# A three-part layer on one core: chunk loads over all partitions, values in one layout, and other tile shapes in the chunk products

## The chip, the cores and the metric

The kernel runs on one core of a Trainium2 chip. The time is device microseconds of that core, the median of three runs; lower is better.

## The reference

Three parts run one after the other on B, S = 4 sequences of 768 tokens, model width 384. First a gated recurrence with 8 heads of width 48, then causal attention in which 4 experts share one input and each token keeps 2 of them, then an MLP with a normalisation. All of it is fp32.

```
state = alpha[:, :, t, :, None] * state + einsum('bhd,bhde->...', k_t, v_t)   # outer product k v
y[:, :, t] = einsum('bhd,bhde->bhe', q_t, state)
...
q, k, v = x @ wq[e], x @ wk[e], x @ wv[e];  a = softmax(causal(q k^T / 8))
out += (e in top 2) * w * ((a @ v) @ wo[e])
...
xn = (x - mu) / sqrt(var + 1e-6) * g_ln;  out = x + relu(xn @ w_ch1) @ w_ch2
```

The change touches the first part alone.

## The kernel before

**The recurrence in chunks.** Each sequence is cut into 6 chunks of 128 tokens, 24 chunks in all, numbered c, with s = c % 6. The 8 heads are 4 pairs: j counts the pairs and h the two heads of a pair. A chunk's alpha, q and k lie in one tile `ld` (four buffers, 128 partitions x 1540 words): head h has partitions 64h to 64h + 47, and the 16 partitions behind them hold ones. The steps of a chunk are:

- `load_sc` (L107) brings alpha, q and k in two transfers of 48 partitions. The ones come once, at the start, in eight transfers of 16 partitions that ACT issues (L132). `load_vn` and `load_vb` bring the same values v twice: `vn` in full and `vb` with one head of the pair in each half of the key rows and zeros elsewhere.
- `gla_a` (L203): DVE scans alpha into the running product `gt` (L215), ACT forms 1/gt by Ln and Exp (L217, L218), DVE and POOL scale k and q by it (L219 to L222).
- `gla_b` (L230): PE forms the scores inside the chunk (L240), DVE masks them into `smk` (L241), PE transposes k (L246) and ACT copies it to `kt` (L248). For scores of head h, the 128 keys are split into two halves of 64, since the second half of the keys meets only the last 64 queries.
- `gla_c` (L252): PE multiplies `kt` by v into the new state (L264), DVE and POOL add it to the old one and scale it (L271 to L274), PE forms the outputs Y from `smk` and v and from q and the old state `st` (L291), ACT and DVE split Y into `xh` and `xl` (L301, L302).

For each two chunks `qkv` projects `xh` and `xl` to the attention's q, k and v (L318, L333). `split_w` (L186) splits the projection weights into WH on ACT and WL on DVE; it runs once, near the start.

**The rest.** Attention goes by units of one 128-query block and one pair of experts: `scores` (L451 on PE, L459 and L463 behind it), `transp` (L485), `av` (L509), `wout` (L522). While the units of the first three sequences run, `conv` splits the MLP's weights, from loads `raw` on SP (L544). The MLP runs last, in `mlp_1` (L642) and `mlp_2` (L659).

**What sets the order.** `front` is a generator that yields an estimated PE time after each step; attention pulls from it so that the chunks are spread between the units. In iteration c of `front` come gla_a(c + 2), gla_b(c + 1), gla_c(c), then the loads for later chunks, then steps of `qkv`. A scheduler then orders each engine's instructions from its own estimate of times; each engine runs its own in that order. All loads but the ones, w1hl and the stores stand in one queue on SP, and an entry there that waits holds up those behind it. PSUM tiles come from one pool of 8 banks (`psf`).

On PE a matmul of fp32 operands is two instructions, and one of fp32r operands is one.

Of the kernel before, what the change touches and what calls it, by code (L numbers as in the profile page):

```python
# [10 lines left out]
F32 = mybir.dt.float32  # L11
# [20 lines left out]
SB = 0  # L32
# [39 lines left out]
def kernel(ctx: ExitStack, tc: tile.TileContext, akq, vt, vd, wqkv, wo, g_ln, w1, w2, ones, out):  # L72
# [30 lines left out]
    vn = [gl.tile([128, 4, 3, 2, 16], F32, name=f"vn{i}") for i in range(3)]  # L103
    vb = [gl.tile([128, 2, 4, 3, 2, 16], F32, name=f"vb{i}") for i in range(2)]
    st = [gl.tile([128, 4, 3, 2, 16], F32, name=f"st{i}") for i in range(2)]

    def load_sc(c):  # L107
        b, s = divmod(c, NSC)
        t = ld[c % 4]
        for h in range(2):  # L110
            sp.dma_start(t[64 * h:64 * h + 48, :], akq[b, s, h])

    def load_vn(c):
        b, s = divmod(c, NSC)
        sp.dma_start(vn[c % 3].rearrange("p j u h e -> p (j u h e)"), vt[b, s])

    def load_vb(c):
        b, s = divmod(c, NSC)
        sp.dma_start(vb[c % 2].rearrange("p x j u h e -> p (x j u h e)"), vd[b, s])
# [26 lines left out]
    load_vn(2)  # L146
# [15 lines left out]
    gmask = gl.tile([128, 192], F32, name="gmask")  # L162
    pool.memset(gmask, -1.0)
    for h in range(2):
        for c0, n in ((0, 128), (128, 64)):
            m = gmask[64 * h:64 * h + 64, c0:c0 + n]
            pool.affine_select(out=m, in_=m, pattern=[[1, n]], compare_op=OP.is_ge, fill=0.0, base=0,
                               channel_multiplier=-1)
# [83 lines left out]
    def gla_c(c):  # L252
        s = c % NSC
        q, k = qk_of(c)
        if s < NSC - 1:
            P = psf()[:, :384].rearrange("p (j u h e) -> p j u h e", j=4, u=3, h=2)
            kt = G.pop((c, "kt"))
            for j in range(4):
                if SB:
                    for h in range(2):  # L260
                        r = slice(64 * h, 64 * h + 64)
                        pe.matmul(P[r, j, :, h, :], kt[:, j, r], vn[c % 3][:, j, :, h, :], start=True, stop=True)
                else:
                    pe.matmul(P[:, j].rearrange("p u h e -> p (u h e)"), kt[:, j, :],  # L264
                              vn[c % 3][:, j].rearrange("p u h e -> p (u h e)"), start=True, stop=True)
            new = st[(c + 1) % 2]
            for h in range(2):
                r = slice(64 * h, 64 * h + 48)
                gl_b = G[c][r, :, 128:129, None].to_broadcast([48, 4, 3, 16])
                if s == 0:  # L270
                    dve.tensor_tensor(new[r, :, :, h, :], P[r, :, :, h, :], gl_b, op=OP.mult)  # L271
# [557 lines left out]
```

## Time and profile before

| | us |
|---|---|
| median of 3 runs (771.96 to 774.6) | 773.7 |
| the profiled execution, its own time | 773.15 |
| span of the profiled execution, first to last instruction | 771.4 |
| PE busy | 719.9 |
| DVE busy | 450.1 |
| ACT busy | 309.9 |
| POOL busy | 186.8 |

Busy times come from the profiled execution. A busy PE counts the modelled ends of pipelined matmuls, so it is not a PE at its peak; how fast matmuls follow each other is read from their start times. What a wait costs is read from the chain of work that ended last, which the page follows back from the last instruction, and from the stage in which the wait stands.

### The profile page before, as it was taken

To read this page: it belongs to the slowest core of one execution; us is meant where nothing else is said; L and a number is where in the kernel's file an instruction comes from. 1 tells how busy PE (TensorE), PEld (TensorE's weight loads), DVE (VectorE), ACT (ScalarE), POOL (GpSimd) and SP (SyncE) were. 2 spreads that over 40 slices of the span, in tenths; PEclk is the share of its full clock that TensorE was granted. 3 is DMA by queue.
4 is the path that set the end of the run, shared out by engine and by line. 5 is a ranking of instruction groups with operands and counts; after the bars stand their busy time and mean duration, and the time that the engine had idled before them with its cause. 6 is when DMAs were issued, how large, how long until landed. Compare 5 with 4: busy or idle time off the path is not lost.

```text
span 771.4 us, 16732 instructions
## 1 busy us (share of the span) xinstructions
PE 719.9 (93%) x6600; PEld 651.6 (84%) x6600; DVE 450.1 (58%) x1349; ACT 309.9 (40%) x903; POOL 186.8 (24%) x311
## 2 busy tenths in 40 slices
PE   3788799889998999999899999999999999999998
PEld 3777588768786778788766898999999999999997
DVE  2767677776877777765579983343354335424521
ACT  2333455544554564545467662331232123222310
POOL 4444345333544424432324320000000000000000
PEclk8697899999999999999999999999999999999999
DMA  9852524345354444221553311011011101110000
GB/s 168 220 146 80 137 92 131 104 109 125 98 161 110 118 121 114 70 85 51 188 210 93 94 52 52 22 31 42 11 33 42 42 11 31 42 39 14 31 21 22
DMA packets 31711, 64.84 MB, mean 84 GB/s; under 512 B 3856, under 2 KB 20752, under 8 KB 31632
## 3 DMA queue, kind: packets, MB, share of 16 engines
q1 hardware_dynamic: 21936, 48.81, 23.6%
q10 hardware_dynamic: 8608, 10.23, 4.4%
q0 software_dynamic: 1088, 4.72, 1.7%
q8 instruction: 52, 0.85, 0.5%
q14 instruction: 27, 0.22, 0.1%
HBM read 49.59 MB, written 14.16 MB: 83 GB/s over the span
## 4 chain that ended last, share of the span: by engine, by line
PE 74%; DMA 11%; DVE 9%; issue 2%; ACT 1%; POOL 1%; SPq 1%; ACTq 0%; DVEq 0%; POOLq 0%
PE F L659 20%; PE F L642 20%; DMA ld<-in_akq_dram 8%; PE F L509 5%; PE F L318 5%; PE F L291 4%; PE F L485 4%; PE F L240 4%; PE F L451 3%; PE F L522 3%; PE F L333 2%; PE F L264 2%; DMA xt<-xs 2%; PE F L246 1%; PE F L623 1%
## 5 line engine op out<-in xcount | busy, mean ns | idle before, releaser
L646 ACT ACTIVATE hh<-F 128x256 fp32r<-128x256 f32 x144 | 54.9, 384 | 202.0 <-PE F L642 201.5
L642 PE MATMUL F<-nh,w1hl 128*128 128x256 f32 x864 | 129.1, 285 | 0.8 <-ACT at L488 0.7
L642 PEld LDWEIGHTS F<-nh,w1hl 128*128 128x128 f32 x864 | 114.7, 191 | 3.1 <-issue 1.0
L659 PE MATMUL F<-w2h,hh 128*128 128x384 f32 x288 | 98.7, 343 | 0.0
L659 PE MATMUL F<-w2l,hh 128*128 128x384 f32 x288 | 97.8, 339 | 0.0
L659 PE MATMUL F<-w2h,hl 128*128 128x384 f32 x288 | 97.7, 339 | 0.0
L647 DVE SCALAR_TENSOR_TENSOR hl<-F,hh 128x256 fp32r<-128x256 f32 x144 | 60.0, 420 | 53.8 <-ACT hh L646 53.7
L463 ACT ACTIVATE A<-F,nm 128x384 f32<-128x384 f32 (+4 forms) x128 | 68.4, 542 | 50.8 <-DVE nm L461 22.8
L663 DVE TENSOR_TENSOR xt<-F,xt 128x384 f32<-128x384 f32 x24 | 13.4, 558 | 112.6 <-PE F L659 112.6
L642 PE MATMUL F<-nl,w1hl 128*128 128x256 f32 x432 | 75.5, 283 | 0.0
L509 PE MATMUL F<-at,V 128*64 128x128 f32 x672 | 59.7, 290 | 5.6 <-DVE rb L511 3.6
L642 PEld LDWEIGHTS F<-nl,w1hl 128*128 128x128 f32 x432 | 62.2, 192 | 0.2 <-DVE cva L548 0.2
L509 PEld LDWEIGHTS F<-at,V 128*64 128x64 f32 x672 | 41.0, 140 | 19.3 <-issue 5.6
L240 PE MATMUL F<-ld 48*64 48x128 f32 (+1 forms) x768 | 44.4, 261 | 13.7 <-DVE ld L221 13.7
L485 PE MATMUL F<-ident,A 128*128 128x128 f32 x336 | 54.2, 283 | 1.9 <-DVE smk L241 1.1
L240 PEld LDWEIGHTS F<-ld 48*64 48x64 f32 x768 | 38.4, 142 | 20.4 <-issue 16.1
L659 PEld LDWEIGHTS F<-w2l,hh 128*128 128x128 f32 x288 | 54.1, 188 | 0.4 <-issue 0.4
L659 PEld LDWEIGHTS F<-w2h,hh 128*128 128x128 f32 x288 | 54.1, 188 | 0.5 <-issue 0.4
L659 PEld LDWEIGHTS F<-w2h,hl 128*128 128x128 f32 x288 | 54.0, 188 | 0.2 <-issue 0.2
L459 DVE CUSTOM_DVE_ANT_0 F<-F,cmask 128x384 f32<-128x384 f32 (+4 forms) x96 | 46.4, 518 | 4.0 <-PE F L451 3.6
L215 DVE TENSOR_TENSOR_SCAN gt<-ld,hot 128x516 f32<-128x516 f32 (+1 forms) x26 | 30.1, 1166 | 30.6 <-DMA ld<-in_akq_dram 20.3
L222 POOL TENSOR_TENSOR ld<-ld,gt 128x512 f32<-128x512 f32 (+1 forms) x26 | 29.8, 1148 | 69.2 <-DVE gt L215 45.9
(246 smaller groups left out, 1433.3 us busy)
## 6 DMA issues: line engine op xcount, KB each, us to landing
ld<-in_akq_dram SPq DMA_DIRECT2D x48, 288.8 KB, 5.8
vb<-in_vd_dram SPq DMA_DIRECT2D x24, 384.0 KB, 3.7
vn<-in_vt_dram SPq DMA_DIRECT2D x24, 192.0 KB, 2.7
raw<-in_w_dram SPq DMA_DIRECT2D x18, 256.0 KB, 2.7
wsc<-whl ACTq DMA_DIRECT2D x18, 256.0 KB, 2.6
xs<-xo ACTq DMA_DIRECT2D x24, 192.0 KB, 1.9
w1hl<-wsc POOLq DMA_DIRECT2D x4, 1152.0 KB, 12.0
raw<-in_w_dram SPq DMA_DIRECT2D x12, 384.0 KB, 3.2
```

The costliest lines, as they stand in the source:

```text
L215: dve.tensor_tensor_scan(gt[:, js].rearrange("p j t -> p (j t)"), al[:, 129 * j0:129 * j1], hot[:, js].rearrange("p j t -> p (j t)"), 0.0, ...
L240: pe.matmul(P[64 * h:64 * h + 64, a, c0:c0 + n], k[r, j, s0:s0 + 64], q[r, j, t0:t0 + n], start=True, stop=True)
L291: pe.matmul(l[x][2], l[x][0], l[x][1], start=(x == 0), stop=(x == n - 1), skip_group_check=True)
L318: pe.matmul(P, wt[:, k, cs], x[:, k], start=(n == 0), stop=(n == 8))
L459: dve.tensor_tensor_reduce(t, t, cmask[:, 512 - pw:], -1.0, 3e38, OP.add, OP.min, m)
L463: act.activation(A[h][:, pw * x:pw * x + pw], t, AF.Exp, bias=nm[:, h:h + 1], scale=1.0 if x < npc - 1 else -1.0, accum_out=dn2[:, h, x:x ...
L485: pe.transpose(P[:, 128 * n:128 * n + 128], A[h][:, 128 * x:128 * x + 128], ident)
L509: pe.matmul(O[64 * h:64 * h + 64, :], V[:, x, HD * e:HD * e + HD], at[:, c:c + 128], start=(x == 0), stop=(x == i), skip_group_check=True)
L642: pe.matmul(P, w[:, k, c], x[:, k], start=(n == 0), stop=(n == 8))
L646: act.activation(hh, P, AF.Relu)
L647: dve.scalar_tensor_tensor(hl, P, 0.0, f(hh), op0=OP.max, op1=OP.subtract)
L659: pe.matmul(P, x[:, o], w[:, ff], start=(ff == 0 and n == 0), stop=(ff == KF - 1 and n == 2))
```

## The change

Values are loaded once, 128 keys on 128 partitions: for each pair j a block x = 0 with the first 32 columns of v of both heads, and a block x = 1 with the last 16 columns of head h in place h of 32 and zeros beside them. `vn` is gone and `vb` has three buffers of 128x512 words in place of two of 128x768. The ones are part of `akq` in memory, so `ld` arrives in one transfer of 128 partitions and ACT issues no load at the start. A chunk's scores are eight matmuls with 48 rows and 128 columns of weights, two heads side by side in two PSUM banks, and the masked scores have 128x512 words per head in place of four blocks of 192 columns. The state product has 128 moving columns in place of 96, and the state is kept in blocks of 32 columns. All outputs are 32 columns of weights wide, four of them side by side. `perm` orders the rows of the projection weights to match.

```diff
     def load_sc(c):
         b, s = divmod(c, NSC)
-        t = ld[c % 4]
-        for h in range(2):
-            sp.dma_start(t[64 * h:64 * h + 48, :], akq[b, s, h])
-
-    def load_vn(c):
-        b, s = divmod(c, NSC)
-        sp.dma_start(vn[c % 3].rearrange("p j u h e -> p (j u h e)"), vt[b, s])
+        sp.dma_start(ld[c % 4], akq[b, s])
...
-    for i in range(4):
-        for cs in ((slice(0, AW), slice(AW, CW)) if i == 0 and AF0 else (slice(0, CW),)):
-            for h in range(2):
-                act.dma_start(ld[i][64 * h + 48:64 * h + 64, cs], ones[:, cs])
-                if i < 2:
-                    sp.dma_start(ld[i][64 * h:64 * h + 48, cs], akq[0, i, h][:, cs])
+    for i in range(2):
+        load_sc(i)
     for i in range(2):
         load_vb(i)
-        load_vn(i)
-        if i == 0:
-            load_sc(2)
...
-    load_vn(2)
+    load_sc(2)
+    load_vb(2)
     load_sc(3)
...
-        SM[c] = gw.tile([128, 4, 192], F32, name="smk")
-        for j0 in (0, 2):
-            P = psf()[:, :384].rearrange("p (j t) -> p j t", j=2)
-            for a in range(2):
-                j = j0 + a
-                for c0, n, s0, t0 in ((0, 128, 0, 0), (128, 64, 64, 64)):
-                    for h in range(2):
-                        r = slice(64 * h, 64 * h + 48)
-                        pe.matmul(P[64 * h:64 * h + 64, a, c0:c0 + n], k[r, j, s0:s0 + 64], q[r, j, t0:t0 + n], start=True, stop=True)
-            dve.tensor_tensor(SM[c][:, j0:j0 + 2], P, gmask[:, None, :].to_broadcast([128, 2, 192]), op=OP.mult)
-            yield 850
+        SM[c] = gw.tile([128, 2, 4, 128], F32, name="smk")
+        P = [psf().rearrange("p (j t) -> p j t", j=4) for h in range(2)]
+        for j in range(4):
+            for h in range(2):
+                r = slice(64 * h, 64 * h + 48)
+                pe.matmul(P[h][:, j], k[r, j], q[r, j], start=True, stop=True)
+            if j == 1:
+                yield 850
+        for h in range(2):
+            dve.tensor_tensor(SM[c][:, h], P[h], gmask[:, None, :].to_broadcast([128, 4, 128]), op=OP.mult)
+        yield 850
...
-                    pe.matmul(P[:, j].rearrange("p u h e -> p (u h e)"), kt[:, j, :],
-                              vn[c % 3][:, j].rearrange("p u h e -> p (u h e)"), start=True, stop=True)
+                pe.matmul(P[:, 128 * j:128 * j + 128], kt[:, j, :], v[:, j].rearrange("p x h e -> p (x h e)"), start=True, stop=True)
+            P = P.rearrange("p (j b e) -> p j b e", j=4, b=4)
...
+                bs = slice(h, 3, 2 - h)
...
-                    dve.tensor_tensor(new[r, :, :, h, :], st[c % 2][r, :, :, h, :], P[r, :, :, h, :], op=OP.add)
-                    (dve if GST else pool).tensor_tensor(new[r, :, :, h, :], new[r, :, :, h, :], gl_b, op=OP.mult)
+                    dve.tensor_tensor(new[r, :, bs], st[c % 2][r, :, bs], P[r, :, h::2], op=OP.add)
+                    (dve if GST else pool).tensor_tensor(new[r, :, bs], new[r, :, bs], gl_b, op=OP.mult)
...
-                l = [(bd[:, 0, j].rearrange("p u h e -> p (u h e)")[:, cs], SM[c][:, j, 0:128], o),
-                     (bd[:, 1, j].rearrange("p u h e -> p (u h e)")[:, cs], SM[c][:, j, 128:192], o[:, 64:128])]
-                if s:
-                    l.append((sto[:112, j, cs], q[:112, j, :], o))
...
         for T in range(2):
-            grp([(2 * T + a, slice(0, 64), Y[64 * a:64 * a + 64, T, :]) for a in range(2)])
+            jobs = []
+            for n in range(4):
+                j, h = 2 * T + n // 2, n % 2
+                l = [(v[:, j, 0, h], sm[:, h, j])]
+                if s:
+                    l.append((sto[:112, j, h], q[:112, j]))
+                jobs.append((Y[32 * n:32 * n + 32, T], l))
+            grp(jobs)
             yield 800
-        grp([(j, slice(64, 96), Y[32 * j:32 * j + 32, 2, :]) for j in range(4)])
+        jobs = []
+        for j in range(4):
+            l = [(v[:, j, 1, h], sm[:, h, j]) for h in range(2)]
+            if s:
+                l.append((sto[:112, j, 2], q[:112, j]))
+            jobs.append((Y[32 * j:32 * j + 32, 2], l))
+        grp(jobs)
...
-            if c + 2 < NCH:
-                load_vb(c + 2)
             if c + 3 < NCH:
-                load_vn(c + 3)
+                load_vb(c + 3)
```

The scheduler's order moves with it. In rows of it, a name's number tells the buffer (`ld_83` is the `ld` of chunks 0, 4, 8 and so on, `ld_85` that of 2, 6, 10), what follows it is the shape, and the last number is how many times in a row. Line numbers are those of the kernel that the row is of. SP's queue at the start of the program, before:

```order
L134 DMA ld_83<-in_akq_dram 48x1540 x2
L134 DMA ld_84<-in_akq_dram 48x1540 x2
L119 DMA vb_90<-in_vd_dram 128x768
L115 DMA vn_87<-in_vt_dram 128x384
L111 DMA ld_85<-in_akq_dram 48x1540 x2
L119 DMA vb_91<-in_vd_dram 128x768
L115 DMA vn_88<-in_vt_dram 128x384
L144 DMA A<-in_wqkv_dram 128x772 x3
L115 DMA vn_89<-in_vt_dram 128x384
L111 DMA ld_86<-in_akq_dram 48x1540 x2
```

And of the changed kernel:

```order
L108 DMA ld_83<-in_akq_dram 128x1540
L108 DMA ld_84<-in_akq_dram 128x1540
L112 DMA vb_87<-in_vd_dram 128x512
L112 DMA vb_88<-in_vd_dram 128x512
L130 DMA A<-in_wqkv_dram 128x772 x3
L108 DMA ld_85<-in_akq_dram 128x1540
L112 DMA vb_89<-in_vd_dram 128x512
L108 DMA ld_86<-in_akq_dram 128x1540
L136 DMA gsb<-in_g_ln_dram 128x3
```

The load of chunk 2 has moved behind the three weight tiles. DVE's order a little later, around the scan (L215) and last product (L221) of chunk 2, before:

```order
L215 SCALAR_TENSOR_TENSOR gt<-ld_85,hot 128x516
L221 SCALAR_TENSOR_TENSOR ld_83<-ld_83 128x256
L220 TENSOR_TENSOR ld_84<-ld_84,gi 128x256
L221 SCALAR_TENSOR_TENSOR ld_83<-ld_83 128x256
L221 SCALAR_TENSOR_TENSOR ld_84<-ld_84 128x256 x2
L241 TENSOR_TENSOR smk<-F,gmask 128x384
L220 TENSOR_TENSOR ld_85<-ld_85,gi 128x512
L189 TENSOR_TENSOR WL<-A,WH 128x772
L241 TENSOR_TENSOR smk<-F,gmask 128x384
L221 SCALAR_TENSOR_TENSOR ld_85<-ld_85 128x512
```

And of the changed kernel, where L199, L204 and L205 are the scan and the two products and L225 is the mask:

```order
L173 TENSOR_TENSOR WL<-A,WH 128x772
L225 TENSOR_TENSOR smk<-F,gmask 128x512 x2
L173 TENSOR_TENSOR WL<-A,WH 128x772
L199 SCALAR_TENSOR_TENSOR gt<-ld_85,hot 128x516
L225 TENSOR_TENSOR smk<-F,gmask 128x512 x2
L252 TENSOR_TENSOR st_91<-F,gt 48x4x2x32
L252 TENSOR_TENSOR st_91<-F,gt 48x4x64
L204 TENSOR_TENSOR ld_85<-ld_85,gi 128x512
L287 TENSOR_TENSOR xl<-F,xh 128x3x128
L199 SCALAR_TENSOR_TENSOR gt<-ld_86,hot 128x516
L205 SCALAR_TENSOR_TENSOR ld_85<-ld_85 128x512
```

The scan of chunk 2 stands behind all of the weight splits now, and its last product behind chunk 1's masks and state and chunk 3's scan. On PE, one chunk in the middle of a sequence (chunk 4), from the last of its scores to its outputs, before:

```order
L240 MATMUL F<-ld_83 64x64 x2
L246 MATMUL F<-ident,ld_83 128x128 x4
L264 MATMUL F<-vn_87,kt 128x96 x4
L291 MATMUL F<-smk,vb_91 64x128 x2
L291 MATMUL F<-smk,vb_91 64x64 x2
L291 MATMUL F<-ld_86,st_93 64x128 x2
L291 MATMUL F<-smk,vb_91 64x128 x2
L291 MATMUL F<-smk,vb_91 64x64 x2
L291 MATMUL F<-ld_86,st_93 64x128 x2
L291 MATMUL F<-smk,vb_91 32x128 x4
L291 MATMUL F<-smk,vb_91 32x64 x4
L291 MATMUL F<-ld_86,st_93 32x128 x4
```

And of the changed kernel (the shape is that of the output; L221, L230, L244 and L263 stand for L240, L246, L264 and L291):

```order
L221 MATMUL F<-ld_83 128x128 x8
L230 MATMUL F<-ident,ld_83 128x128 x4
L244 MATMUL F<-vb_87,kt 128x128 x4
L263 MATMUL F<-smk,vb_87 32x128 x4
L263 MATMUL F<-ld_86,st_91 32x128 x4
L263 MATMUL F<-smk,vb_87 32x128 x4
L263 MATMUL F<-ld_86,st_91 32x128 x4
L263 MATMUL F<-smk,vb_87 32x128 x8
L263 MATMUL F<-ld_86,st_91 32x128 x4
```

The scores come as eight matmuls where sixteen stood, and the 64-column outputs and the products with 64 moving columns are gone.

## Rows read from the trace of the kernel before

**Rows 1.** The page's chain that ended last: share of the span by engine.

```profile
PE 74%; DMA 11%; DVE 9%; issue 2%; ACT 1%; POOL 1%; SPq 1%; ACTq 0%; DVEq 0%; POOLq 0%
```

**Rows 2.** Windows: us, busy of PE, PEld, DVE, ACT, POOL, clock, DMA, GB/s.

```profile
0.00:25.00 25.00, 8.78 (x56) 8.39 (x56) 9.97 (x14) 6.82 (x13) 11.54 (x27) 0.80 0.96 214
...
50.00:92.00 42.00, 31.71 (x374) 26.84 (x373) 30.23 (x86) 15.83 (x46) 20.09 (x30) 0.85 0.52 129
92.00:372.00 280.00, 265.79 (x3030) 223.49 (x3029) 203.12 (x626) 142.16 (x422) 110.55 (x190) 0.98 0.39 105
```

**Rows 3.** Chain in order of time: start us, us, what.

```profile
2.18 10.26 DMA ld<-in_akq_dram
12.46 8.02 DMA ld<-in_akq_dram
...
39.38 4.61 PE F L318 x36
...
50.76 7.18 DMA ld<-in_akq_dram
...
75.46 6.51 DMA ld<-in_akq_dram
...
260.18 5.64 DMA ld<-in_akq_dram
```

**Rows 4.** Timeline of the start: start us, us, instruction, idle before and releaser.

```profile
0.85 11.46 ACTq L132 DMA_DIRECT2D ld<-in_ones_dram  x8
...
8.17 1.28 DVE L215 TENSOR_TENSOR_SCAN gt<-ld,hot 128x258 f32<-128x258 f32 x2 [8.17 <-DMA ld<-in_ones_dram]
...
12.36 0.73 ACT L217 ACTIVATE gi<-gt 128x258 f32<-128x258 f32 x2 [10.26 <-DMA ld<-in_ones_dram]
...
22.41 1.54 PE L240 MATMUL F<-ld 48*64 48x128 f32 x16 [12.59 <-DVE ld L221]
```

**Rows 5.** The page's DMA issues: count, KB each, us to landing.

```profile
ld<-in_akq_dram SPq DMA_DIRECT2D x48, 288.8 KB, 5.8
...
vn<-in_vt_dram SPq DMA_DIRECT2D x24, 192.0 KB, 2.7
```

**Rows 6.** Windows of two stretches at the start, columns as in rows 2.

```profile
3.00:15.00 12.00, 6.82 (x40) 6.58 (x38) 2.86 (x5) 2.20 (x7) 4.87 (x13) 1.00 1.04 186
20.50:25.00 4.50, 1.54 (x16) 1.39 (x16) 4.40 (x5) 2.74 (x4) 2.57 (x2) 0.50 1.10 400
```

**Rows 7.** Window from the first scan to chunk 3's scan.

```profile
8.10:34.70 26.60, 12.93 (x148) 11.75 (x148) 18.16 (x27) 8.31 (x16) 10.68 (x10) 0.68 0.94 215
```

**Rows 8.** Waits: who for whom, us in total, times, longest.

```profile
DVE gt L215 <- DMA ld<-in_akq_dram: 20.3, 9, 3.4
```

**Rows 9.** Timeline of PE in two stretches.

```profile
191.87 0.28 PE L451 MATMUL F<-KH,QL 64*128 64x128 f32 x2
191.98 0.28 PE L451 MATMUL F<-KL,QH 64*128 64x128 f32 x2
...
258.13 0.54 PE L291 MATMUL F<-smk,vb 128*32 128x128 f32 x16
258.48 0.41 PE L291 MATMUL F<-ld,st 112*32 112x128 f32 x8
```

**Rows 10.** Chain in order of time, 250 to 262 us.

```profile
252.78 1.49 PE F L240 x32
...
254.85 0.87 PE F L264 x8
```

**Rows 11.** Window of the PE stage, instructions of L240 alone.

```profile
92.00:372.00 280.00, 30.09 (x544) 25.61 (x544) 0.98 0.39 105
```

**Rows 12.** Chain of the PE stage, shares by line.

```profile
by line: DMA ld<-in_akq_dram 11.2%; PE F L318 9.8%; PE F L291 8.8%; PE F L509 8.4%; PE F L240 6.4%; PE F L485 6.1%; PE F L451 5.7%; PE F L333 5.1%; PE F L522 4.6%; PE F L264 3.9%; issue 3.3%; PE F L246 2.1%; DMA raw<-in_w_dram 2.0%; DVE F L
```

**Rows 13.** Groups by form, 0 to 440 us: busy us, mean ns.

```profile
L241 DVE TENSOR_TENSOR smk<-F,gmask 128x384 f32<-128x384 f32 x48 | 25.9, 548 | 1.2 <-PE F L240 0.9
...
L490 DVE COPY at<-F 128x512 f32<-128x512 f32 x17 | 11.6, 682 | 0.4 <-PE F L485 0.3
```

More of the change, by code (lines that the diff above doesn't have):

```diff
@@ L71, with kernel @@
 @with_exitstack
-def kernel(ctx: ExitStack, tc: tile.TileContext, akq, vt, vd, wqkv, wo, g_ln, w1, w2, ones, out):
+def kernel(ctx: ExitStack, tc: tile.TileContext, akq, vd, wqkv, wo, g_ln, w1, w2, out):
     nc = tc.nc
@@ L102 @@
     ld = [gl.tile([128, CW], F32, name=f"ld{i}") for i in range(4)]
-    vn = [gl.tile([128, 4, 3, 2, 16], F32, name=f"vn{i}") for i in range(3)]
-    vb = [gl.tile([128, 2, 4, 3, 2, 16], F32, name=f"vb{i}") for i in range(2)]
-    st = [gl.tile([128, 4, 3, 2, 16], F32, name=f"st{i}") for i in range(2)]
+    vb = [gl.tile([128, 4, 2, 2, 32], F32, name=f"vb{i}") for i in range(3)]
+    st = [gl.tile([128, 4, 3, 32], F32, name=f"st{i}") for i in range(2)]
     def load_sc(c):
         b, s = divmod(c, NSC)
-        t = ld[c % 4]
-        for h in range(2):
-            sp.dma_start(t[64 * h:64 * h + 48, :], akq[b, s, h])
-    def load_vn(c):
-        b, s = divmod(c, NSC)
-        sp.dma_start(vn[c % 3].rearrange("p j u h e -> p (j u h e)"), vt[b, s])
+        sp.dma_start(ld[c % 4], akq[b, s])
     def load_vb(c):
         b, s = divmod(c, NSC)
-        sp.dma_start(vb[c % 2].rearrange("p x j u h e -> p (x j u h e)"), vd[b, s])
+        sp.dma_start(vb[c % 3].rearrange("p j x h e -> p (j x h e)"), vd[b, s])
     def new_gen(b):
@@ L161 @@
         pool.memset(t, 0.0)
-    gmask = gl.tile([128, 192], F32, name="gmask")
+    gmask = gl.tile([128, 128], F32, name="gmask")
     pool.memset(gmask, -1.0)
-    for h in range(2):
[L165 to L168, printed above, removed]
+    pool.affine_select(out=gmask, in_=gmask, pattern=[[1, 128]], compare_op=OP.is_ge, fill=0.0, base=0,
+                       channel_multiplier=-1)
     cmask = const.tile([128, 512], BF, name="cmask")
@@ L254, in gla_c @@
         q, k = qk_of(c)
+        v = vb[c % 3]
         if s < NSC - 1:
-            P = psf()[:, :384].rearrange("p (j u h e) -> p j u h e", j=4, u=3, h=2)
+            P = psf()
             kt = G.pop((c, "kt"))
             for j in range(4):
[L259 to L263, printed above, removed]
-                    pe.matmul(P[:, j].rearrange("p u h e -> p (u h e)"), kt[:, j, :],
-                              vn[c % 3][:, j].rearrange("p u h e -> p (u h e)"), start=True, stop=True)
+                pe.matmul(P[:, 128 * j:128 * j + 128], kt[:, j, :], v[:, j].rearrange("p x h e -> p (x h e)"), start=True, stop=True)
+            P = P.rearrange("p (j b e) -> p j b e", j=4, b=4)
             new = st[(c + 1) % 2]
@@ L275, in gla_c @@
             yield 850
         Y = psf()[:, :384].rearrange("p (k t) -> p k t", k=3)
-        bd = vb[c % 2]
-        sto = st[c % 2].rearrange("p j u h e -> p j (u h e)")
+        sm, sto = SM.pop(c), st[c % 2]
         def grp(jobs):
-            ops = []
-            for j, cs, o in jobs:
-                l = [(bd[:, 0, j].rearrange("p u h e -> p (u h e)")[:, cs], SM[c][:, j, 0:128], o),
-                     (bd[:, 1, j].rearrange("p u h e -> p (u h e)")[:, cs], SM[c][:, j, 128:192], o[:, 64:128])]
-                if s:
-                    l.append((sto[:112, j, cs], q[:112, j, :], o))
-                ops.append(l)
-            n = len(ops[0])
-            for x in range(n):
-                for l in ops:
-                    pe.matmul(l[x][2], l[x][0], l[x][1], start=(x == 0), stop=(x == n - 1), skip_group_check=True)
@@ L293, in gla_c @@
-        for T in range(2):
-            grp([(2 * T + a, slice(0, 64), Y[64 * a:64 * a + 64, T, :]) for a in range(2)])
-            yield 800
-        grp([(j, slice(64, 96), Y[32 * j:32 * j + 32, 2, :]) for j in range(4)])
+            for x in range(max(len(l) for o, l in jobs)):
+                for o, l in jobs:
+                    pe.matmul(o, l[x][0], l[x][1], start=(x == 0), stop=(x == len(l) - 1), skip_group_check=True)
+        for T in range(2):
+            jobs = []
+            for n in range(4):
+                j, h = 2 * T + n // 2, n % 2
+                l = [(v[:, j, 0, h], sm[:, h, j])]
+                if s:
+                    l.append((sto[:112, j, h], q[:112, j]))
+                jobs.append((Y[32 * n:32 * n + 32, T], l))
+            grp(jobs)
+            yield 800
@@ L793, in _layout @@
         for h in range(2):
-            for u in range(3):
-                for e in range(16):
-                    d = (2 * j + h) * D + u * 16 + e
-                    row = (j // 2) * 128 + 64 * (j % 2) + 32 * u + 16 * h + e if u < 2 else 256 + 32 * j + 16 * h + e
-                    perm[row] = d
+            for d in range(D):
+                row = 128 * (j // 2) + 64 * (j % 2) + 32 * h + d if d < 32 else 256 + 32 * j + 16 * h + d - 32
+                perm[row] = (2 * j + h) * D + d
     wq, wk, wv = (np.asarray(inp['moe_' + n]) for n in ('wq', 'wk', 'wv'))
@@ L808, in _layout @@
     return {n: np.ascontiguousarray(a) for n, a in
-            (('akq', akq), ('vt', vt), ('vd', vd), ('wqkv', wqkv), ('wo', wo), ('g_ln', g), ('w1', w1), ('w2', w2),
-             ('ones', np.ones((16, CW), np.float32)))}
+            (('akq', akq), ('vd', vd), ('wqkv', wqkv), ('wo', wo), ('g_ln', g), ('w1', w1), ('w2', w2))}
 def kernel(**inputs):
```

27 lines of the change are left out of this document (13 added, 14 removed).

## The prediction

> **What bounds the kernel now.** I read the chain that ended last first. PE carries 74% of it, DMA 11%, DVE 9% [rows 1]. The last 331 us of the span (the MLP) contain nothing that this change touches, so the question is what happens before 440 us, and there the stages differ. The windows by stage [rows 2] show it: from 0 to 25 us PE is busy 8.78 us, at a mean granted clock of 0.80; from 50 to 92 it is busy 31.7 of 42 us; from 92 to 372, where chunks of the recurrence and attention units are interleaved, it is busy 265.8 of 280 us. So the start is bound by something that PE waits for, 50 to 92 partly so, and 92 to 372 is a PE stage.
>
> In order of time the chain names what is waited for [rows 3]: two loads of `ld` fill it from 2.2 to 20.5 us, and later single loads of `ld` of 5.6 to 7.2 us stand in it, seven in all, of which the rows show the first two and the last. The timeline of the start [rows 4] shows why: ACT issues its eight loads of ones from 0.85 to 12.3 us and can only then begin the Ln of chunk 0 (12.36), although DVE had the first scan at 8.17; PE's first score follows at 22.41.
>
> **The start.** The eight ACT loads disappear, and `ld` of chunk 0 becomes the first transfer on SP with nothing beside it on the other queue. What does it cost? One `ld` half is 288.8 KB on 48 partitions [rows 5], so the new load of 128 partitions is 770 KB, or 788 thousand bytes. Two rates stand in the trace with the DMA engines full [rows 6]: 186 GB/s from 3 to 15 us, when halves of `ld` and ones were moving, and 400 GB/s from 20.5 to 25 us, when the `wqkv` tiles and a `vn`, all on 128 partitions, had been issued. Neither is the new transfer; it has the partitions of the second and the row length of the first. I take the second, since row lengths of 1.5 and 3 KB ran side by side at that rate, so that length alone did not set it, and keep the first as a rival. The fixed part: a `vn` load of 192 KB lands 2.7 us after its issue [rows 5]; 0.5 of that is its bytes at 400 GB/s, so 2.2 us. The first `ld` would land at 0.8 + 2.2 + 2.0 = 5.0 us, chunk 1 two microseconds later, and, after 0.5 MB of values and 1.2 MB of weights, chunk 2 at about 14.
>
> From there DVE sets the pace, by the order above: the new order has all three WL splits and chunk 1's masks ahead of chunk 2's last product (L205). Before, DVE was busy 18.16 us from 8.1 to 34.7 us [rows 7], which is this same work up to the scan of chunk 3. Adding 4 x 0.14 us for wider masks (below), 0.6 for one more subtraction and 1.2 us of waits for Ln and Exp gives 5.0 + 18.2 + 1.1 + 1.2 = 25.5 us. [...] **The start saves 8.9 us**; 5.0 at the slow DMA rate (rival A), 13 if DVE's waits and PE's clock turn out better.
>
> **The later loads of `ld`.** A lone load now takes 0.4 (one issue) + 2.2 + 2.0 = 4.6 us, or 5.3 with the 256 KB of `vb` ahead of it. The chain has 7.18 and 6.51 us in the stage that is not PE-bound: I count 2.5 and 2.0, **4.5 us** (0 to 7). The other five lie in the PE stage; at 1 to 2.5 us each they could give 8, but there other work takes over when a wait shrinks, and the whole time that DVE's scan waited for these loads is 20.3 us in 9 waits [rows 8] over the kernel. I take **3 us** (0 to 8).
>
> **PE's own work per chunk.** I need the spacing of fp32 passes (each fp32 matmul is two instructions). Pairs of 64-row, 128-column tiles with 128 columns moving follow each other after 0.11 us, both halves of the array at once (L451 at 191.87 and 191.98), though in fp32r, one pass; and 16 instructions of four-wide 128x32 tiles, half with 128 and half with 64 columns, take 0.35 us [rows 9], so a four-wide set costs 0.11 us with 128 columns and 0.06 with 64. The chunk scores (L240) take 1.49 us and the state products (L264) 0.87 for 8, that is 0.11 each [rows 10]: 16 passes of 0.11 and 0.056 in equal number are 1.33 us, so about 0.15 us of the 1.49 is spent where the shape of tile changes.
> - Scores: 8 pairs of passes x 0.11 = 0.88 against 1.33 us: -0.45.
> - State products: 96 columns become 128 at 0.11 us each: the 96-column ones already take that, so 0, at worst +0.2.
> - Outputs: 14 four-wide passes x 0.11 = 1.54, against three groups of 4 passes of 0.11 and 2 of 0.056, 1.65: -0.10.
> - The outputs no longer go from 64- to 32-column tiles halfway: one change of shape less, -0.15. Over the whole order the changes of shape go from 370 to 346.
>
> That is -0.70 us per chunk. In 92 to 372 us there are 544/32 = 17 chunks [rows 11], 11.9 us of PE time. What share of it is on the path? In that stage the chain has L240 for 6.4% of 280 us, 17.9 us [rows 12], of 17 x 1.49 = 25.3: 0.71. So **8.5 us** (0 to 11.9).
>
> **What it adds.** DVE's mask product goes from 384 to 512 columns: 548 ns now, and a PSUM copy of 512 columns takes 682, so +0.14 us, twice a chunk. The state sum goes from 192 to 256 elements, by the same slope +0.07, twice [rows 13]. Together 0.41 x 17 = 7 us of DVE time in the PE stage, where DVE is busy 203 of 280. A third of it on the path: **+2 us** (0 to 7). POOL's product for the state gets longer too; POOL has 1% of the chain, so I count nothing, and if that cover goes it is under 0.2 us a chunk. One new neighbour on POOL: chunk 2's gm waits behind g20, which waits for `gsb`, now the eleventh transfer on SP; at 400 GB/s it lands near 17 us, before chunk 2's scan is done.
>
> **Sum.** -8.9 - 4.5 - 3 - 8.5 + 2 = -22.9. The profiled span is 771.4 us and its own time 773.15, so 1.75 us lie around it; the median of the runs is 0.55 above that. 771.4 - 22.9 + 1.75 + 0.55 = **751 us**.
>
> **Rivals.**
> A. The big load runs at 186 GB/s, because the long rows and not the 48 partitions are slow. Then chunk 2 lands at 25 us, and 4.5 us of scan, Ln, Exp, products and 5 of PE put the first projection at 34.4 (saves 5.0); the later loads take 0.4 + 2.2 + 4.2 and save nothing: -5.0 - 8.5 + 2 gives 762. For it: no transfer of 6 KB rows on 128 partitions is in the trace. Against: 1.5 and 3 KB rows shared the fast rate. [...] Chance 0.13.
> B. The PE time that is freed was not on the path, since another engine's result is waited for in its place: without the 8.5 us, 759. For it: DVE is in order and 73% busy there; against: PE at 95%. 0.12.
> C. The weight loads of the 128-column tiles don't overlap, so that the 16 score passes take 0.11 each one after another, 1.76 us: +0.18 per chunk instead of -0.70, 762. Against it stand the L451 pairs, which have the same tile. [...] 0.05.
> D. Slower: PE idles more and its granted clock falls. From 50 to 92 us, with PE 75% busy, it was 0.85 [rows 2]; from 92 to 372, 0.98. If the shorter chunks open gaps there, 266 us of PE work stretch: at 0.90 by 23.7 us, which eats all of the gain, and at 0.88 by 30, which ends at 781. Against it: PE keeps attention's matmuls to fill with. 0.07.
> The change doing nothing measurable, by a mixture of these, gets 0.03.
>
> **Chances and range.** The forecast has 0.60 (742 to 758 by itself). A, B and C end at 759 to 762, still faster. The low end, with the start at -13, loads at -7 and -8, PE at -11.9 and nothing for DVE, would be 734; all of that together is unlikely, 736 is my lower bound. Upwards A with part of B and DVE's full 7 us is 767. A difference under 0.3% (2.3 us) can't be told from none. Faster 0.90, same 0.03, slower 0.07.
>
> **What would show it.** Right: the first scan near 5 us, the first score near 11, the first projection near 30; `ld` landing in under 5 us with DMA rates near 400 GB/s while it moves; the score line at about 0.9 us per chunk, the state line unchanged, output four-wide at 1.5 us; DVE's mask at 0.69 us. Wrong: `ld` landing after 6 us or more (A); score passes one after another (C); PE idle in 92 to 372 grown by as much as its work shrank (B), a granted clock there under 0.9 (D), or a new wait of POOL for `gsb` ahead of chunk 2.

## The result, and the profile after

The changed kernel takes 751.56 us (median of 4 runs) beside 774.15 us of the kernel before on the same chip: ratio 0.972 [0.968, 0.977]. A second measurement on another chip (e11 below) gave 0.974 [0.970, 0.977]. Against the kernel before, measured beside it each time, that is 22.6 and 19.9 us less. The profiled execution has a span of 749.9 us and an own time of 751.59.

In the changed kernel the lines move up: the scan is L199, Ln and Exp L201 and L202, the scores L221, the mask L225, transposes L230, state products L244, outputs L263, `xh` L286, the first projection L303. The windows by stage, columns as in [rows 2]:

```profile
0.00:25.00 25.00, 15.20 (x120) 13.04 (x120) 19.05 (x27) 9.97 (x18) 13.27 (x26) 0.83 0.69 264
50.00:92.00 42.00, 36.85 (x404) 30.60 (x397) 33.92 (x101) 19.33 (x59) 18.06 (x30) 0.88 0.37 125
92.00:372.00 280.00, 264.85 (x2904) 221.07 (x2902) 212.96 (x659) 147.95 (x443) 122.19 (x201) 0.97 0.35 115
```

Beside [rows 2], PE is busy 6.4 us longer by 25 us and 5.1 us longer between 50 and 92. From 92 to 372 it is as busy as before, but now holds more of the program. The page's DMA issues, which answer to [rows 5]:

```profile
ld<-in_akq_dram SPq DMA_DIRECT2D x24, 770.0 KB, 4.7
vb<-in_vd_dram SPq DMA_DIRECT2D x24, 256.0 KB, 2.7
```

and the window of the first five microseconds in which the DMA engines are full, which answers to [rows 6]:

```profile
3.00:8.00 5.00, 5.00 (x33) 5.00 (x32) 2.13 (x4) 1.46 (x4) 2.52 (x8) 1.00 1.00 397
```

One load of 770 KB now lands sooner after its issue than one of 288.8 KB did. At the start the DMA engines move 397 GB/s, where they moved 186 with the old loads. The waits of DVE's scan for `ld` shrink from 20.3 us [rows 8] to

```profile
DVE gt L199 <- DMA ld<-in_akq_dram: 7.3, 4, 5.1
```

of which 5.1 is the very first load. (Before, DVE's first wait of 8.17 us was put down to the ones [rows 4] and is not in the 20.3; without the first wait the two are 20.3 and 2.2.) The timeline of the start (start us, us, instruction, idle before and releaser), beside [rows 4] and the 39.38 of [rows 3]:

```profile
5.08 1.28 DVE L199 TENSOR_TENSOR_SCAN gt<-ld,hot 128x258 f32<-128x258 f32 x2 [5.08 <-DMA ld<-in_akq_dram]
...
10.95 0.71 PE L221 MATMUL F<-ld 48*128 48x128 f32 x8 [2.02 <-DVE ld L205]
...
16.86 0.94 DVE L173 TENSOR_TENSOR WL<-A,WH 128x772 fp32r<-128x772 f32 x1
17.73 1.22 DVE L199 TENSOR_TENSOR_SCAN gt<-ld,hot 128x516 f32<-128x516 f32 x1
...
25.84 2.08 PE L221 MATMUL F<-ld 48*128 48x128 f32 x16 [5.34 <-issue]
...
31.75 0.40 PE L263 MATMUL F<-ld,st 112*32 112x128 f32 x8
...
32.35 1.23 DVE L199 TENSOR_TENSOR_SCAN gt<-ld,hot 128x516 f32<-128x516 f32 x1 [0.96 <-POOL st L255]
33.62 0.63 ACT L201 ACTIVATE gi<-gt 128x516 f32<-128x516 f32 x1 [4.01 <-DVE gt L199]
34.28 0.63 ACT L202 ACTIVATE gi<-gi 128x516 f32<-128x516 f32 x1
34.83 0.47 ACT L286 ACTIVATE xh<-F 128x384 fp32r<-128x384 f32 x1
35.35 0.62 PE L303 MATMUL F<-xh,WH 128*128 128x256 f32 x3 [3.19 <-ACT xh L286]
```

The first scan and first score come where they were forecast (5.0 and 11), but the first projection starts at 35.35 and not at 30.5 (39.4 - 8.9). PE has finished chunk 1's outputs by 32.15; `xh` would follow, but on ACT it stands behind Ln and Exp of chunk 4, whose scan has just waited for POOL. So ACT, idle for 4.01 us until 33.62, leaves `xh` standing from 32.15 on and then does two other instructions first. When the 1st, 3rd, 7th, 9th and 12th projection start in the timelines, as the difference to the kernel before (us; minus is earlier; a projection is the work of `qkv` for two chunks; the kernels e1 to e11 come below, and e11 is the changed kernel itself, profiled a second time):

| projection | before, at | changed | e11 | e1 | e6 | e5 | e2 | e9 |
|---|---|---|---|---|---|---|---|---|
| 1 | 39.4 | -4.0 | -3.8 | -11.6 | -3.1 | -11.6 | +5.3 | -0.7 |
| 3 | 91.2 | -11.4 | -11.0 | -13.5 | -4.5 | -16.2 | +1.7 | -4.8 |
| 7 | 226.2 | -21.5 | -18.8 | -14.6 | -7.5 | -27.0 | -4.7 | -7.7 |
| 9 | 301.2 | -22.6 | -22.3 | -18.4 | -11.4 | -24.6 | +2.5 | -5.6 |
| 12 | 364.1 | -21.8 | -21.1 | -18.4 | -11.4 | -23.7 | +3.0 | -5.5 |

Each column is one execution. Two of the same kernel, changed and e11, differ by 0.2 and 0.4 us at the first and third projection and by 2.7 at the seventh, so small differences in the lower rows mean little.

PE's timeline of one chunk of the changed kernel at full clock:

```profile
46.98 1.16 PE L221 MATMUL F<-ld 48*128 48x128 f32 x16
48.08 0.66 PE L230 MATMUL F<-ident,ld 128*128 128x128 f32 x4
48.57 1.06 PE L244 MATMUL F<-vb,kt 128*128 128x128 f32 x8
49.55 0.43 PE L263 MATMUL F<-smk,vb 128*32 128x128 f32 x8
49.80 0.40 PE L263 MATMUL F<-ld,st 112*32 112x128 f32 x8
...
50.90 0.41 PE L263 MATMUL F<-ld,st 112*32 112x128 f32 x8
```

From start to start, the scores with their change of shape take 1.10 us (before 1.49 [rows 10]) and the state products 0.98; the outputs take 1.35 to the start of their last group. The timeline of before has, at full clock too, 0.96 for the state products (254.69 to 255.65) and 1.61 for the outputs up to their last group (36.76 to 38.37):

```profile
36.76 0.55 PE L291 MATMUL F<-smk,vb 128*64 128x128 f32 x8
...
38.37 0.40 PE L291 MATMUL F<-ld,st 112*32 112x128 f32 x8
...
254.69 1.03 PE L264 MATMUL F<-vn,kt 128*128 128x96 f32 x8
255.65 0.55 PE L291 MATMUL F<-smk,vb 128*64 128x128 f32 x8
```

The mask product, 548 ns before [rows 13], is 0.68 us in the groups by form from 92 to 372 us (busy us, mean ns):

```profile
L225 DVE TENSOR_TENSOR smk<-F,gmask 128x512 f32<-128x512 f32 x32 | 21.2, 680 | 0.3 <-PE F L221 0.3
```

### The profile page after: what moved, and what is told of

Its sections match the earlier page's. It is cut to its first block, busy times and chain, and to the rows that moved or that the text cites. A ratio compares the mean times of both kernels' runs of the same rounds, so it can differ in the third digit from the quotient of the medians.

```text
span 749.9 us, 16151 instructions
## 1 busy us (share of the span) xinstructions
PE 710.6 (95%) x6376; PEld 641.1 (85%) x6376; DVE 457.1 (61%) x1349; ACT 309.9 (41%) x903; POOL 191.9 (26%) x308
## 3 DMA queue, kind: packets, MB, share of 16 engines
q1 hardware_dynamic: 18864, 45.68, 18.5%
## 4 chain that ended last, share of the span: by engine, by line
PE 53%; DVE 2%; DMA 2%; ACT 1%; POOL 1%; issue 0%; ACTq 0%; POOLq 0%; DVEq 0%
PE F L642 20%; PE F L625 20%; PE F L492 3%; PE F L468 2%; PE F L434 2%; DMA raw<-in_w_dram 2%; PE F L505 2%; PE F L303 1%; PE F L606 1%; PE F L318 1%; ACT A L446 0%; DVE F L442 0%; DMA wsc<-whl 0%; POOL cva L543 0%; PE F L483 0%
## 5 line engine op out<-in xcount | busy, mean ns | idle before, releaser
L221 PE MATMUL F<-ld 48*128 48x128 f32 x384 | 40.4, 306 | 10.4 <-issue 5.3
L221 PEld LDWEIGHTS F<-ld 48*128 48x128 f32 x384 | 32.6, 201 | 17.0 <-issue 8.9
L468 PEld LDWEIGHTS F<-ident,A 128*128 128x128 f32 x336 | 38.5, 145 | 9.4 <-issue 4.9
L471 ACT ACTIVATE at<-F 128x512 f32<-128x512 f32 (+1 forms) x72 | 38.1, 536 | 15.6 <-PE F L468 9.5
```

Of the source, the lines that this page charges most:

```text
L221: pe.matmul(P[h][:, j], k[r, j], q[r, j], start=True, stop=True)
L468: pe.transpose(P[:, 128 * n:128 * n + 128], A[h][:, 128 * x:128 * x + 128], ident)
L471: act.activation(at[:, cs], P[:, :128 * len(g)], AF.Copy)
```

## The experiments

The theory was that the two parts of the change add up: the loads give the start and the waits for `ld`, the shapes give PE time of which 0.7 is on the path. Its rivals were those of the prediction. The result raised two more questions: why the first projection was 4.9 us late against the forecast, and whether rows or partitions make a load fast. Ratios are to the kernel before, measured beside each; the last column is median minus median.

| kernel | loads | shapes | chunk 2's `ld` | ratio, 95% | us |
|---|---|---|---|---|---|
| e1 | new | old | early | 0.976 [0.973, 0.979] | -18.2 |
| e6 | new | old | late | 0.985 [0.981, 0.989] | -11.6 |
| e2 | old | new | late | 0.998 [0.996, 1.001] | -1.6 |
| e9 | old | new | early | 0.993 [0.990, 0.996] | -5.9 |
| changed | new | new | late | 0.972 and 0.974 | -22.6, -19.9 |
| e5 | new | new | early | 0.965 [0.962, 0.969] | -26.0 |

"Early" is between the first two loads of `vb`, as in the kernel before; "late" is behind the `wqkv` tiles, as in the change. "New shapes" stands for PE's tile shapes together with the values in one layout: no run parts these two, and what is called the shapes' gain below holds both.

**e1: the loads alone.** The kernel before, with

```
-        t = ld[c % 4]
-        for h in range(2):
-            sp.dma_start(t[64 * h:64 * h + 48, :], akq[b, s, h])
+        sp.dma_start(ld[c % 4], akq[b, s])
...
-                act.dma_start(ld[i][64 * h + 48:64 * h + 64, cs], ones[:, cs])
...
```

> The kernel before with one part of the change: q, k, gates and the ones as one load of 128 partitions on SP, no loads of ones on ACT; values in two layouts and all tile shapes of PE as before. Theory (the terms of the prediction add up, the two parts separate): the gain of the start, 4 us at the first projection, and some 7 us more up to 92 us appear here, 2 to 3 us of later ld waits as well, so 774 - 13 = 761 us, between 759 and 765. Rival (the freed PE time of the new shapes is not on the path, all the gain is the loads'): 752 us. First scan near 5 us and ld landing in under 5 us by both.

Measured: 757.89 us. Most of the gain is the loads', more than expected, but 752 it is not. The first scan is at 5.45, but an `ld` lands 6.0 us after its issue and not in under 5, and DVE waits 12.0 us for `ld` in all (changed kernel: 4.7 and 7.3). Beside each `ld`, e1 still loads `vb` of 384 KB and `vn` of 192 KB, where the changed kernel loads 256 KB of values; a part of what the new shapes gain may be this. The surprise is the table of projections: the first comes at 27.7, 7.6 us ahead of the changed kernel, which has the same load and less PE work.

**e2: the shapes alone.** The changed kernel with the old loads:

```
-        sp.dma_start(ld[c % 4], akq[b, s])
+        t = ld[c % 4]
+        for h in range(2):
+            sp.dma_start(t[64 * h:64 * h + 48, :], akq[b, s, h])
...
+            act.dma_start(ld[i][64 * h + 48:64 * h + 64, :], ones)
...
```

> The changed kernel with the old loads put back: two ld loads of 48 partitions and eight loads of ones issued by ACT; values in one layout and PE's new tile shapes stay. Theory: only the 0.70 us per chunk of PE time times its share of the path appears, 774 - 8.5 = 765 us, between 762 and 768. Rival (freed PE time not on the path): 772 to 775 us. A third way: if the two parts need each other (a shorter chunk only helps once the loads are early), this run and the one with the loads alone give together clearly less than 22 us.

Measured: 774.51 us, which the theory missed and the rival had. The third way is left open: e1 and e2 give 19.8 us together, as much as the second measurement of the whole change. The table shows how it comes about: 5.3 us are lost by the first projection, 10 gained from there to the seventh, and 7.7 lost again behind it. The first loss made the place of chunk 2's load suspect, since e1 still had it early. e5, e6 and e9 test that.

**e5: the changed kernel with chunk 2's load early.**

```
     for i in range(2):
         load_vb(i)
+        if i == 0:
+            load_sc(2)
...
-    load_sc(2)
     load_vb(2)
```

> The changed kernel with one load moved: ld of chunk 2 is issued between the two first vb loads, where it stood before the change, and not behind the wqkv tiles. Theory (the change loses 4 to 8 us at the start because chunk 2's load went behind the weights, so that DVE has all three WL splits ahead of chunk 2's scan: with the new load alone the first projection came at 27.8 us, with the whole change at 35.35): scan of chunk 2 near 14 us in place of 17.7, first projection at 28 to 31 us, and 3 to 6 us less in all, 746 to 749. Rival (a start that comes earlier is given back before 92 us, where PE waits for later ld loads and xh): first projection earlier, fourth projection where it was, 750 to 753.

Measured: 748.70 us, as the theory had it. Its timeline of the start (lines one higher than in the changed kernel):

```profile
13.39 1.22 DVE L200 TENSOR_TENSOR_SCAN gt<-ld,hot 128x516 f32<-128x516 f32 x1
...
18.47 0.95 DVE L174 TENSOR_TENSOR WL<-A,WH 128x772 fp32r<-128x772 f32 x1
...
21.57 1.16 PE L222 MATMUL F<-ld 48*128 48x128 f32 x16
...
27.30 0.47 ACT L287 ACTIVATE xh<-F 128x384 fp32r<-128x384 f32 x1
...
27.83 0.62 PE L304 MATMUL F<-xh,WH 128*128 128x256 f32 x3 [1.94 <-ACT xh L287]
```

Chunk 2's scan now stands ahead of all three WL splits on DVE, where in the changed kernel it stood behind them (17.73 after the last at 16.86). Chunk 2's scores are 4.3 us earlier, and `xh` of chunk 1 no longer waits behind chunk 4's Ln. The edit moves one transfer and nothing else; the scheduler, which orders each engine by its own estimate of times, moved DVE's and ACT's work with it.

**e6: the mirror, e1 with chunk 2's load late.**

```
         load_vn(i)
-        if i == 0:
-            load_sc(2)
...
+    load_sc(2)
     load_vn(2)
```

> The mirror: the kernel with the new load alone (e1), but with ld of chunk 2 issued behind the wqkv tiles as the whole change has it. Theory: first projection later than e1's 27.8 by 4 to 7 us, time 761 to 764 against e1's 758. Rival (what makes the first projection late in the changed kernel is its longer DVE work or PE's new tiles, not the place of the load): within 1 us of e1.

Measured: 763.09 us against e1's 757.89, the first projection at 36.3 and not 27.7: 8.5 us later, where 4 to 7 were expected. The old shapes lose at least as much by the late load as the new ones do, so neither DVE's longer products nor PE's tiles are what made the start late.

**e9: the missing corner, old loads, new shapes, chunk 2's load early.** The edit is that of e5, in e2.

> The kernel with the new shapes and values but the old loads (e2), and with ld of chunk 2 issued between the first two vb loads as before the change: the missing corner of loads x shapes x place of chunk 2's load. Theory (the shapes are worth 9 us by themselves, as from e1 to e5, and e2 showed 1.6 only because it also had chunk 2's load behind the weights): 765 to 769. Rival (with the old loads PE's freed time is not on the path, PE waits for ld anyway): 772 to 775.

Measured: 768.74 us, 5.9 less than before: the shapes are worth something by themselves, at the edge of the theory's range. By the medians they are worth less than with the new loads (e1 to e5: 7.8; e6 to changed: 8 to 11), but with intervals of about 2.3 us to either side of each ratio that is not shown. The windows of the PE stage, of e9 and then of e2:

```profile
92.00:372.00 280.00, 264.61 (x2880) 220.81 (x2878) 209.67 (x638) 142.64 (x420) 119.61 (x196) 0.95 0.32 84
```

```profile
92.00:372.00 280.00, 264.45 (x2848) 220.76 (x2849) 209.49 (x634) 141.78 (x417) 116.50 (x193) 0.94 0.33 88
```

PE's mean granted clock there is 0.95 and 0.94, with 0.98 before [rows 2] and 0.97 in the changed kernel. DVE still waits for `ld` in seven (e9) and eight (e2) places, 17.4 and 14.5 us in all. Which of the two makes the shapes worth less there, if they are, no run shows.

**e4: `xh` first on ACT.** The changed kernel, with

```
+    XA = (4, 6)
...
+            with (tc.issue_after(XHI[c - 3].ins) if c in XA else ExitStack()):
+                act.activation(gi[:, js], gt[:, js], AF.Ln)
+                act.activation(gi[:, js], gi[:, js], AF.Exp, scale=-1.0)
...
+        XHI[c] = act.activation(xh[:, :, o], Y, AF.Copy)
```

> The changed kernel with Ln and Exp of chunks 4 and 6 queued on ACT behind the xh of chunks 1 and 3; nothing else is moved. Theory (the start gained 4 us and not 8.9 because xh of chunk 1 stands on ACT behind chunk 4's Ln and Exp, whose scan comes late): the first projection starts at 32.5 to 33 us in place of 35.35, the projection behind chunk 3 some 2 us earlier than 53.8, and the time falls by 2 to 4 us, to 748 to 750. Rival (PE goes on with work that it had anyway, or chunk 4's gates are then late by as much as xh is early): first projection earlier, but the second and third projections where they were, time 751 to 752.

Measured: ratio 0.965 [0.961, 0.968], median 749.30. Its timeline (lines three higher):

```profile
32.13 0.49 ACT L289 ACTIVATE xh<-F 128x384 fp32r<-128x384 f32 x1 [2.46 <-PE F L266]
...
32.67 0.62 PE L306 MATMUL F<-xh,WH 128*128 128x256 f32 x3 [0.61 <-ACT xh L289]
```

`xh` starts when PE's outputs are done, the projection 2.7 us earlier, and the profiled execution is still 3.1 us ahead of the changed one at the last projection. ACT's order did hold the path there.

**e10: both repairs.** The edits of e4 and e5 together.

> Both repairs of the start together: chunk 2's load early (e5) and Ln and Exp of chunks 4 and 6 on ACT behind xh of chunks 1 and 3 (e4). In e5 xh of chunk 1 already stood ahead of chunk 4's Ln; only that of chunk 3, for which PE waited 4.5 us until 49.05, stands behind chunk 6's Ln and Exp of 1.3 us. Theory: 1 to 2 us less than e5, 746.5 to 748. Rival (PE takes up that wait elsewhere before 92 us): as e5, 748 to 749.5.

Measured: 747.88 us, ratio 0.967 [0.964, 0.970]. The median is 0.8 us below e5's and within the theory's range, but the ratio of e5 is 0.965: the two can't be told apart, as the rival said. The second projection is 2.3 us earlier than in e5, the third is 0.3 us later: PE takes the wait up before 92 us. Each of e4, e5 and e10 has a lower median and ratio than the changed kernel, with intervals below that of its second measurement, and among the three the runs show no order.

**e3: the load in two halves.** The changed kernel, with

```
-        sp.dma_start(ld[c % 4], akq[b, s])
+        for h in range(2):
+            sp.dma_start(ld[c % 4][64 * h:64 * h + 64, :], akq[b, s, 64 * h:64 * h + 64])
```

> The changed kernel with its ld load issued as two DMAs of 64 partitions each, same bytes and same row length. If the slow rate of the old load came from how few partitions a transfer covers, and two halves on one queue don't make up for it, ld of chunk 0 is complete later than 5 us by 1 to 2 us, the first scan starts at 6 to 7 us and the time rises by 1 to 4 us, 753 to 756. If rows of 6 KB go at full rate whatever the partitions of one transfer, since both halves move side by side, only the second issue of 0.4 us on SP is added: first scan near 5.5, time within 1 us of the changed kernel's 751.6.

Measured: 768.03 us, ratio 0.991 [0.988, 0.994], far above both expectations: about 60% of the gain are gone. The first scan starts at 7.38, later still than the 6 to 7 us of the first expectation. What was not expected is that the delay then comes again with later chunks: DVE waits 19.8 us for `ld` in place of 7.3.

**e7: the same, even and odd partitions.**

```
-        sp.dma_start(ld[c % 4], akq[b, s])
+        for h in range(2):
+            sp.dma_start(ld[c % 4][h:128:2, :], akq[b, s, h:128:2])
```

> The changed kernel with its ld load in two DMAs of 64 partitions each, as in e3, but one takes the even and the other the odd partitions, so that each spans all 128; bytes, rows and count of DMAs as in e3. If what counts is how far over the 128 partitions a transfer reaches, this lands as the whole load does (complete before 5.5 us, first scan 5.1 to 5.6) and the time is 751 to 754. If what counts is how many partitions one DMA has, it is as slow as e3: first scan at 7.4, 766 to 770.

Measured: 756.27 us, ratio 0.976 [0.971, 0.981], 2 us above the first expectation and far from the second. The first scan is at 5.72, just behind the 5.1 to 5.6 expected, and DVE waits 11.6 us for `ld` (e3: 19.8, changed kernel: 7.3). e3 and e7 have the same count of DMAs of 385 KB, the same rows and the same bytes. The windows from 3 to 8 us and the page's DMA queue (packets, MB, share of 16 engines' span), of e3:

```profile
3.00:8.00 5.00, 5.00 (x26) 5.00 (x25) 0.62 (x2) 0.00 (x0) 0.89 (x6) 1.00 1.01 233
```

```profile
q1 hardware_dynamic: 19248, 45.68, 22.3%
```

and of e7:

```profile
3.00:8.00 5.00, 5.00 (x26) 5.00 (x25) 1.48 (x3) 1.38 (x4) 2.38 (x8) 1.00 0.93 318
```

```profile
q1 hardware_dynamic: 19248, 45.68, 18.8%
```

The same 19248 packets took 22.3% of the engines' time in one and 18.8% in the other (changed kernel: 18864 packets, 18.5%). So of two loads with the same bytes, the same rows and 64 partitions per DMA, the one whose DMAs spread over all 128 partitions moved 318 GB/s and the one on neighbouring partitions 233; neither row length nor the number of partitions in one DMA made this difference. What makes it, and why e7 has 318 and not 397 GB/s in these first microseconds, with the DMA engines busy 0.93 of the time, no run shows; from 8 to 15 us it moves 413, the changed kernel 417 and e3 331. In time e7 can't be told from the changed kernel by the ratios; its median is some us higher, and whether that is the second issue on SP stays open.

**e8: PE time put back.** The changed kernel with work added that the result doesn't need:

```
             P = psf()
+            for x in range(8):
+                pe.transpose(P[:, 128 * (x % 4):128 * (x % 4) + 128], k[:, x % 4, :], ident)
             for j in range(4):
```

> The changed kernel with PE work added: in each of the 20 chunks that have transposes, eight more transposes of the same k tile into the same PSUM tile ahead of the four (written over by them), 8 x 0.11 = 0.88 us a chunk at full clock, about what the new shapes save. Theory (0.7 of PE's time per chunk is on the path): 13 such chunks lie in the stage from 92 to 372 us, 13 x 0.88 x 0.71 = 8 us, and part of the 6 earlier ones, so 8 to 13 us, 760 to 765. Rival (PE has slack, its freed time is not on the path): under 3 us, 751 to 754.

Measured: 764.54 us, ratio 0.987 [0.983, 0.992], in the theory's range and far from the rival's. Against the changed kernel that is 10 to 12 us more for 20 x 0.93 = 18.6 us of PE time, a share of 0.53 to 0.67. One chunk's rows, and the window of the PE stage:

```profile
106.09 1.09 PE L230 MATMUL F<-ident,ld 128*128 128x128 f32 x8
107.03 0.60 PE L232 MATMUL F<-ident,ld 128*128 128x128 f32 x4
107.46 1.06 PE L246 MATMUL F<-vb,kt 128*128 128x128 f32 x8
```

```profile
92.00:372.00 280.00, 267.19 (x3013) 226.02 (x3011) 209.50 (x642) 143.84 (x429) 119.82 (x200) 1.00 0.32 104
```

The eight added transposes (L230) take 0.94 us to the next group here, and 0.93 in most chunks of the trace, where 0.88 was expected. The mean clock of the stage is 1.00 with the added work and 0.97 without, so part of the changed kernel's work ran at a lower clock than e8's, and the share may be too small by that; how much is not measured.

**e11: the changed kernel again.**

> The changed kernel once more, unaltered, beside the two others on the same chip: 750 to 754, so that e5, e9 and e10 can be set against it.

Measured: 754.78 us, a little above the range; the ratio of 0.974 [0.970, 0.977] lies within the interval of the first measurement. In its profile the clock falls in another place than in the first one. The window from 160 to 170 us, of the first profile of the changed kernel and then of e11:

```profile
160.00:170.00 10.00, 8.96 (x122) 7.99 (x123) 6.66 (x20) 5.52 (x15) 4.75 (x7) 1.00 0.69 231
```

```profile
160.00:170.00 10.00, 8.93 (x99) 7.38 (x100) 6.30 (x17) 5.03 (x13) 4.28 (x5) 0.66 0.65 206
```

PE is busy for as long in both, but does fewer matmuls at the lower clock, and from the fifth to the sixth projection e11 takes 28.0 us where the first profile took 25.2.

## Why the prediction was right, point by point

**The time (751 forecast, 751.6 measured) is right, but its terms are not.** The start gave 4.9 us less than forecast, the two stages behind it 2.9 and 1.7 more. That these made up for each other almost to the microsecond is luck.

- *The start, -8.9:* the step that failed. It measured -4.0. Of the working, 5.0 for the first load, 11 for the first score and 25.5 for the end of DVE's chain are right (5.08, 10.95, 25.84). Behind them the forecast has 5.0 us to the first projection (39.4 - 8.9 = 30.5), 4.5 for PE and 0.5 on ACT for `xh`: this was the author's estimate, and no run shows it. The runs showed 6.3 us of PE, with a granted clock of 0.50 from 23.5 to 30 us (the 16 score passes took 2.08 us there and 1.16 at full clock), where PE stood idle for 5.34 us until 25.84; and on ACT they showed Ln and Exp of chunk 4 ahead of `xh`. That queue cost 2.7 us (e4). 0.3 + 1.8 + 2.7 is 4.8 of the 4.9.
- *The moved load:* the prediction followed where chunk 2's load went, but priced it only inside the sum and not by itself. e5 and e6 do: left where it was, it is worth 3.4 to 6.6 us. "DVE sets the pace, by the order above" was true, and the order was a choice of the change.
- *50 to 92 us, -4.5:* from the first to the third projection 7.4 us were gained. Part of this may be the start's: e1, whose first projection was not late, gains only 1.9 there. But e1 also waits longer for `ld`: DVE's waits for it between 36 and 92 us were 5.8 us before, 4.6 in e1 and 0.6 in the changed kernel. How much of the 7.4 is which, no run parts.
- *The PE stage, -8.5 - 3 + 2 = -9.5:* from the third to the ninth projection 11.2 us. The loads alone give 4.9 (e1) or 6.9 (e6) of this, where 3 was forecast; the shapes add 3.5 (e1 to e5) or 4.3 (e6 to changed), where -8.5 + 2 was forecast. Over the whole kernel the shapes give 7.8 us (e1 to e5) or 8 to 11 (e6 to changed). PE saves per chunk, by the rows above, 0.39 on the scores with their change of shape, 0.26 on the outputs with theirs, and loses 0.02 on the state products: 0.63 where 0.70 was forecast. What was short is the count: the 17 chunks of one stage were priced, and the shapes act on all 24. By the third projection they have already given 2.7 us (e1 to e5) or 6.9 (e6 to changed). All 24 chunks at 0.63 and the share of e8 give 8.0 to 10.1 us before DVE's part; that is worked out and not measured by itself, and the values' one layout is in what was measured.
- *The share on the path, 0.71:* e8 has 0.53 to 0.67, somewhat less, with intervals wide enough to hold 0.71.
- *DVE, +2:* the mask is 0.68 us (0.69 forecast); what of it is on the path no run tells apart.
- *The time of a load:* `ld` lands 4.7 us after its issue (4.6 forecast).

**The rivals.** A is refuted by 397 GB/s, and e3 and e7 (233 GB/s on neighbouring partitions, 318 on spread ones; 186 before) make it likely that the old loads were slow by the narrow stretch of partitions that each covered. B is refuted by e8 and by e1 against e5. C is refuted: 16 score passes and the change of shape take 1.10 us, not 1.76 and more. D did not happen to the forecast size (0.97 in the stage, 0.98 before), but a fall of the clock behind a less busy stretch is there: from 200 to 210 us PE was busy for 7.75 of 10 us, and from 210 to 220 its clock was 0.55. That the one made the other is not shown. e2 and e9, with short chunks and old loads, have the lowest clock of the stage (0.94, 0.95). POOL did not wait for `gsb`, which landed 8.2 us after its issue at 7.64 and was read at 20.32.

What stays open is how much such falls of the clock take from the gain. The changed kernel and e5 gain nothing more behind the seventh projection (-21.5 to -21.8, -27.0 to -23.7), while e1 gains 3.8 there, and their clock from 210 to 240 us is 0.83 and 0.80, with 1.00 in e1 and before. e11 is the same kernel as the changed one, with 0.89 there, and gains 2.3 behind the seventh projection; what it had lost instead is the 2.8 us between the fifth and the sixth. So where the clock falls differs from one execution to the next and goes with about this much time, but no run takes the falls away.

## What to carry to other kernels

Price each moved load by what the scheduler then puts behind it on every engine: here one transfer, moved past three weight tiles, took 3 to 7 us from a change that gave 20 to 23. At the end of a forecast chain, read the queue of the engine that does the last short step, not only the step. Where two parts of a change are to be told apart, run all corners: the shapes alone seemed worth nothing (1.6 us), because the late load of chunk 2 was in that run too; without it they were worth 5.9.

## What the runs showed of the hardware

Two DMAs of 64 neighbouring partitions on one queue moved at 233 GB/s from 3 to 8 us, with the DMA engines busy 1.01 of the time, where the same bytes on even and odd partitions moved at 318 (busy 0.93) and in one DMA at 397 (1.00); the neighbouring halves did not make up for each other. So for a load cut in two it mattered which partitions each half took. PE's granted clock over the PE stage was 1.00 with eight more transposes per chunk and 0.97 without, but it did not simply follow PE's work: e1, with more PE work than the changed kernel (266.8 us busy there against 264.9), has 0.97 as well. And two executions of the changed kernel had their clock fall at different places: 0.66 from 160 to 170 us in one, where the other has 1.00 at the same busy share (8.93 and 8.96 of 10 us).
